# Gated linear attention and an MLP mixer on one core: transposes by crossbar DMA, inputs by casting DMA

## The chip, the cores and the metric

The kernel runs on one core of a Trainium2 chip. The metric is device time in microseconds (us), from one launch of the whole program. The core has TensorE (PE, matmuls, and its weight loads PEld), VectorE (DVE), ScalarE (ACT), GpSimd (POOL) and SyncE (SP). SP does nothing here but issue DMAs by the hardware queue; POOL issues DMAs by the software queue and also computes. All DMAs of the core run on the same 16 DMA engines.

## What is computed

For each of 4 batches and 8 heads, with S = 768 steps and head size D = 48, a gated recurrence runs over the steps, and its output, with the heads side by side (768 x 384), goes through an MLP mixer over tokens and then over channels:

```
f = 1 / (1 + exp(-f_logit))
for t in range(S):
    state = f[t][:, None] * state + outer(k[t], v[t])      # 48 x 48 per head
    y[t]  = q[t] @ state
x  = y with heads side by side                             # 768 x 384 per batch
u  = x + (relu(x.T @ w_tok1) @ w_tok2).T                   # w_tok1 768 x 256, w_tok2 256 x 768
out = u + relu(u @ w_ch1) @ w_ch2                          # w_ch1 384 x 1536, w_ch2 1536 x 384
```

All inputs and the output are float32 in memory.

## The kernel before

The recurrence is done in chunks of 128 steps, so NCH = 6 chunks per batch, steps on the partitions. Within a chunk the gates become a cumulative sum S of log(1 + exp(-f_logit)), and q and k are scaled by exp(-S) and exp(S); what remains is a masked product inside the chunk plus a term from the state carried in.

**Loads.** `load_batch_inputs(b, 1)` (L75) issues, for each chunk, four DMAs of 128 x 8 heads x 48 float32 (1024 rows of 192 bytes each) on SP: f_logit, q, k and v. v goes to one float32 staging tile `v_ld` and is cast to bf16 by POOL (L81). The four MLP weights are loaded whole by POOL (L62 to L65), which casts them to bf16 on the way. The order in the program is batch 0, weights, batch 1 (L298 to L300); batch b + 2 is loaded after batch b's attention (L328). `q_sb`, `k_sb`, `f_sb`, `v_sb` and the log gates `Lhi`, `Llo` (the high and low bf16 halves of the log gate) have two buffers each, by the batch's parity.

**Gates.** `prep_gates_slices` (L118) makes exp, ln and the high half on ACT (L124, L127, L130), and the low half on DVE (L133). Batch 0 does it chunk by chunk (L302 to L304). Batches 1 to 3 do it for all six chunks in one, a step after each of the chunks 1 to 4 of the batch ahead (L322).

**Attention.** `attn_front` (L137) makes the cumulative sum of a chunk in PSUM (`ps_S`, two matmuls) and the chunk's total (`ps_dg`). `attn_chunk` (L153) then takes exp of it both ways on ACT (`G`, `Gi`, L159, L160), scales q on DVE to `qh` (L164) and k on POOL to `kh` (L165). Both are 128 steps x 8 heads x 64 (48 used). PE transposes them in pairs of heads, 4 + 4 blocks of 128 x 128, into the PSUM tile `ps_tr` (L169, L170), and DVE copies the eight blocks to `qkT` in one instruction (L171). The scores `ps_AT` (L176) and their mask `AmT` (L185, L186) follow, then the output `ps_y` (L189, L195), the state's update (`ps_dg` L200, L209 to L215; it reads `kh` as it is, not transposed), and two copies of `ps_y` to `x_nat` (float32) and `x_bf` (L205, L206). `G`, `Gi`, `qh`, `kh`, `qkT` and `AmT` have two buffers by the chunk's parity; `ps_S` and `ps_y` have one.

**MLP.** `moe_slices(b)` (L223) gives six slices for batch b. They are called one each inside the chunks of batch b + 1 (L182), and those of batch 3 at the end: `s_tok` (token mixing, ends with `u_nat` L241 and its bf16 copy `u_bf` L242), `s_ut` (transposes `u_bf`, 18 blocks of 128 x 128, through `ps_moe` and three DVE copies to `uT`, L253 to L255), three times `s_ch` (channel expansion, L265, with the relu on ACT or DVE, L272, L270) and `s_out` (L283, L286, and the store on SP, L287). `ps_moe` has two buffers, and every MLP matmul group uses them.

**Order.** The program gives what depends on what. The tile framework's scheduler sets the order of each engine's instructions at compile time, from its own estimate of their lengths and from their place in the program; at run time each engine, and each of the queues of SP and POOL, works strictly in that order, and waits on semaphores.

Of the kernel before, what the change touches and what calls it, by code (L numbers as in the profile page):

```python
# [9 lines left out]
FP32 = mybir.dt.float32  # L10
BF16 = mybir.dt.bfloat16
_DBG = False
AF = mybir.ActivationFunctionType
ALU = mybir.AluOpType
# [3 lines left out]
def kernel(  # L18
# [12 lines left out]
    nc = tc.nc  # L31
    B, H, S, D = q.shape
    C = 128
    NCH = S // C
    HP = H // 2
# [7 lines left out]
    def st(shape, dtype, tag):  # L43
        return sb.tile(shape, dtype, tag=tag, name=tag)

    def pt(shape, dtype, tag):
        return ps.tile(shape, dtype, tag=tag, name=tag)

    tri_bf = st([128, 128], BF16, "tri_bf")
    ident = st([128, 128], BF16, "ident")  # L50
# [13 lines left out]
        nc.gpsimd.dma_start(out=w_ch1, in_=moe_w_ch1.rearrange("(kt p) n -> p kt n", p=128))  # L64
        nc.gpsimd.dma_start(out=w_ch2, in_=moe_w_ch2.rearrange("(kt p) n -> p kt n", p=128))  # L65

    q_sb = [st([128, H, NCH, D], FP32, f"q_sb{i}") for i in range(2)]
    k_sb = [st([128, H, NCH, D], FP32, f"k_sb{i}") for i in range(2)]
    v_ld = [st([128, H, NCH, D], FP32, "v_ld")] * 2
    v_sb = [st([128, H, NCH, D], BF16, f"v_sb{i}") for i in range(2)]  # L70
    f_sb = [st([128, H, NCH, D], FP32, f"f_sb{i}") for i in range(2)]
    Lhi = [st([128, NCH, H, 64], BF16, f"Lhi{i}") for i in range(2)]
    Llo = [st([128, NCH, H, 64], BF16, f"Llo{i}") for i in range(2)]

    def load_batch_inputs(b, step):  # L75
        i = b % 2
        for c in range(0, NCH, step):
            for dst, src in ((f_sb, f_logit), (q_sb, q), (k_sb, k), (v_ld, v)):
                nc.sync.dma_start(out=dst[i][:, :, c:c + step, :],
                                  in_=src[b].rearrange("h (c t) d -> t h c d", t=C)[:, :, c:c + step, :])  # L80
            nc.gpsimd.tensor_copy(v_sb[i][:, :, c:c + step, :], v_ld[i][:, :, c:c + step, :])  # L81

    G = [st([128, H, 64], BF16, f"G{i}") for i in range(2)]
    Gi = [st([128, H, 64], BF16, f"Gi{i}") for i in range(2)]
    qh = [st([128, H, 64], BF16, f"qh{i}") for i in range(2)]
    kh = [st([128, H, 64], BF16, f"kh{i}") for i in range(2)]
# [15 lines left out]
    nc.vector.memset(state_bd, 0.0)  # L102

    ps_S = pt([128, 512], FP32, "ps_S")
    ps_tr = pt([128, 8, 128], BF16, "ps_tr")
    ps_AT = [pt([128, 4, 128], FP32, f"ps_AT{p}") for p in range(2)]
    ps_y = pt([128, H, D], FP32, "ps_y")
    ps_dg = pt([128, HP, 2 * D + 1], FP32, "ps_dg")
# [9 lines left out]
    def prep_gates_slices(b, c0=0, c1=NCH):  # L118
        ib = b % 2
        fb = f_sb[ib][:, :, c0:c1, :]  # L120
        fbc = f_sb[ib].rearrange("t h c d -> t c h d")[:, c0:c1]

        def g_exp():
            nc.scalar.activation(fb, fb, AF.Exp, bias=0.0, scale=-1.0)  # L124

        def g_ln():
            nc.scalar.activation(fb, fb, AF.Ln, bias=1.0, scale=1.0)  # L127

        def g_hi():
            nc.scalar.activation(Lhi[ib][:, c0:c1, :, 0:D], fbc, AF.Copy, bias=0.0, scale=1.0)  # L130

        def g_lo():
            nc.vector.tensor_tensor(Llo[ib][:, c0:c1, :, 0:D], fbc,  # L133
                                    Lhi[ib][:, c0:c1, :, 0:D], ALU.subtract)
        return [g_exp, g_ln, g_hi, g_lo]
# [17 lines left out]
    def attn_chunk(b, c, mid=(), front_next=None):  # L153
        i = c % 2
        ib = b % 2
        last = c == NCH - 1

        sview = ps_S.rearrange("t (h dd) -> t h dd", dd=64)[:, :, 0:D]
        nc.scalar.activation(G[i][:, :, 0:D], sview, AF.Exp, bias=0.0, scale=-1.0)  # L159
        nc.scalar.activation(Gi[i][:, :, 0:D], sview, AF.Exp, bias=0.0, scale=1.0)  # L160
        if not last:
            nc.scalar.activation(glast, ps_dg[:, :, 2 * D], AF.Exp, bias=0.0, scale=-1.0)

        nc.vector.tensor_tensor(qh[i][:, :, 0:D], q_sb[ib][:, :, c, :], G[i][:, :, 0:D], ALU.mult)  # L164
        nc.gpsimd.tensor_tensor(kh[i][:, :, 0:D], k_sb[ib][:, :, c, :], Gi[i][:, :, 0:D], ALU.mult)  # L165

        qb, kb = blk(qh[i]), blk(kh[i])
        for hp in range(HP):
            nc.tensor.transpose(ps_tr[:, hp, :], qb[:, hp, :], ident)  # L169
            nc.tensor.transpose(ps_tr[:, 4 + hp, :], kb[:, hp, :], ident)  # L170
        nc.vector.tensor_copy(qkT[i], ps_tr)  # L171

        for h in range(H):
            hp, par = h // 2, h % 2
            rows = slice(par * 64, par * 64 + D)
            nc.tensor.matmul(ps_AT[par][:, hp, :], lhsT=qkT[i][rows, 4 + hp, :],  # L176
                             rhs=qkT[i][rows, hp, :], start=True, stop=True)

        if front_next is not None:
            front_next()  # L180
        for m in mid:
            m()  # L182

        tb4 = tri_bf.unsqueeze(1).broadcast_to((128, 4, 128))
        nc.vector.tensor_tensor(AmT[i][:, 0:4, :], ps_AT[0], tb4, ALU.mult)  # L185
        nc.vector.tensor_tensor(AmT[i][:, 4:8, :], ps_AT[1], tb4, ALU.mult)  # L186

        for h in range(H):
            nc.tensor.matmul(ps_y[:, h, :], lhsT=AmT[i][:, (h % 2) * 4 + h // 2, :],  # L189
                             rhs=v_sb[ib][:, h, c, :],  # L190
                             start=(h == 0), stop=(c == 0 and h == H - 1),
                             skip_group_check=True)
        if c > 0:
            for hp in range(HP):
                nc.tensor.matmul(ps_y[:, 2 * hp:2 * hp + 2, :], lhsT=qkT[i][:, hp, :],  # L195
                                 rhs=state_bd[:, hp, :],
                                 start=False, stop=(hp == HP - 1), skip_group_check=True)
        if not last:
            for hp in range(HP):
                nc.tensor.matmul(ps_dg[:, hp, 0:2 * D], lhsT=kb[:, hp, :],  # L200
                                 rhs=v_sb[ib][:, 2 * hp:2 * hp + 2, c, :],
                                 start=True, stop=True)

        yflat = ps_y.rearrange("t h e -> t (h e)")
        nc.scalar.activation(x_nat[ib][:, c, :], yflat, AF.Copy, bias=0.0, scale=1.0)  # L205
        nc.scalar.activation(x_bf[ib][:, c, :], yflat, AF.Copy, bias=0.0, scale=1.0)  # L206

        if not last:
            nc.vector.tensor_tensor(state[0:D], state[0:D], ps_dg[0:D, :, 0:D], ALU.add)  # L209
            nc.vector.tensor_tensor(state[64:64 + D], state[64:64 + D],  # L210
                                    ps_dg[64:64 + D, :, D:2 * D], ALU.add)
            nc.vector.tensor_tensor(state, state, glast.unsqueeze(2).broadcast_to((128, HP, D)),  # L212
                                    ALU.mult)
            nc.vector.tensor_copy(state_bd[0:D, :, 0:D], state[0:D])
            nc.vector.tensor_copy(state_bd[64:64 + D, :, D:2 * D], state[64:64 + D])  # L215
# [7 lines left out]
    def moe_slices(b):  # L223
        ib = b % 2
# [22 lines left out]
        sl.append(s_tok)  # L247

        def s_ut():
            for dmb in range(3):  # L250
                pm = ps_moe[dmb % 2].bitcast(BF16)
                for stt in range(NCH):
                    nc.tensor.transpose(pm[:, stt * 128:(stt + 1) * 128],  # L253
                                        u_bf[:, stt, dmb * 128:(dmb + 1) * 128], ident)
                nc.vector.tensor_copy(uT[:, dmb, :], pm[:, 0:S])  # L255
            if _DBG:
                nc.sync.dma_start(out=dbg_uT[b], in_=uT)
        sl.append(s_ut)
# [32 lines left out]
    if _DBG:  # L291
# [2 lines left out]
        dbg_h1 = nc.dram_tensor("dbg_h1", (B, 128, 2, DM), BF16, kind="Internal").ap()  # L294
        dbg_uT = nc.dram_tensor("dbg_uT", (B, 128, 3, S), BF16, kind="Internal").ap()
        dbg_zT = nc.dram_tensor("dbg_zT", (B, 128, 12, S), BF16, kind="Internal").ap()
    nc.scalar.preload_act_table_set("natural_log_exp_and_others")
    load_batch_inputs(0, 1)  # L298
    load_weights()
    load_batch_inputs(1, 1)  # L300
    prev_moe: list = []
    for c in range(NCH):  # L302
        for g in prep_gates_slices(0, c, c + 1):
            g()  # L304
    for b in range(B):
        ib = b % 2
        attn_batch_begin(b)
        next_gates = prep_gates_slices(b + 1) if b + 1 < B else []
        if b == 0:
            attn_front(b, 0)  # L310
        for c in range(NCH):
            if c + 1 < NCH:
                fn = (lambda cc: (lambda: attn_front(b, cc)))(c + 1)
            elif b + 1 < B:
                fn = lambda: attn_front(b + 1, 0)
            else:
                fn = None
            mid = []
            if c < len(prev_moe):
                mid.append(prev_moe[c])  # L320
            attn_chunk(b, c, mid=mid, front_next=fn)
            if 1 <= c <= len(next_gates):  # L322
                next_gates[c - 1]()
        if _DBG:
            nc.sync.dma_start(out=dbg_x[b].rearrange("(c t) n -> t c n", t=C),
                              in_=x_nat[b % 2])
        if b + 2 < B:
            load_batch_inputs(b + 2, 1)  # L328
        prev_moe = moe_slices(b)
    for s in prev_moe:  # L330
        s()
# [30 lines left out]
```

## Time and profile before

| | us |
|---|---|
| median of the runs (2) | 257.42 |
| lowest, highest | 256.96, 257.89 |
| the profiled execution's own time | 257.89 |
| its span, first to last instruction | 256.1 |
| busy: PE, PEld | 194.3, 113.9 |
| busy: DVE, ACT, POOL | 151.7, 115.1, 39.5 |
| mean granted TensorE clock | 0.947 |

The profile is of one execution. It has the busy time of each engine, the span in 40 equal slices of 6.4 us (a digit is the busy share in tenths), the DMA queues, the costliest groups of instructions, and, on demand, the timeline of an engine, the instructions of one source line, and tables of busy time between given moments. An engine's row with a "q" (SPq, POOLq) is its queue of DMA issues. In a timeline line the first number is the start in us from the span's start, the second the length, and in brackets at the end stands the idle time ahead of it and what ended it. Names such as `kh_96` and `kh_97` are two buffers of one tile; `in_f_logit_dram` is an input.

### The profile page before, as it was taken

The page shows a single profiled execution, that of the slowest core. Times are in us where ns is not written, and L with a number is a line of the kernel's source. Part 1 is how long each engine was busy: PE and PEld are TensorE (multiplying, and loading weights), DVE is VectorE, ACT ScalarE, POOL GpSimd, SP SyncE. Part 2 cuts the span into 40 slices and gives each one's busy share as a digit, 9 for nine tenths or more (in the row PEclk, how much of TensorE's full clock was granted, in tenths as well). Part 3 has the DMA queues.
Part 4 walks back from the last instruction along what each step waited for, and adds up shares of the span by engine and source line. Part 5 has one row for each costly group of instructions (what it writes and reads, how often), then busy time and mean ns, then how long its engine had stood idle before and what let it go on. Part 6 is the DMA issues. An engine that isn't in the chain of part 4 may idle for free. (4 is left out here: it accounts for less than half of the span.)

```text
span 256.1 us, 4360 instructions
## 1 busy us (share of the span) xinstructions
PE 194.3 (76%) x1678; PEld 113.9 (44%) x1688; DVE 151.7 (59%) x321; ACT 115.1 (45%) x240; POOL 39.5 (15%) x60
## 2 busy tenths in 40 slices
PE   0300168676795885899988989999799999789994
PEld 0100036452342444566654546665466566344462
DVE  4200059894631499976699998438998842542231
ACT  4502055424469554491485976017465601635300
POOL 1420062401010242301222231001210100000000
PEclk9999999976897798589999999999999999999999
DMA  7999999999999998019999000121000012000022
GB/s 141 165 208 189 193 186 178 189 178 176 179 195 189 168 166 140 0 32 198 227 167 181 5 0 3 61 92 35 0 4 0 3 61 96 29 0 0 3 92 92
DMA packets 106324, 27.02 MB, mean 105 GB/s; under 512 B 100288, under 2 KB 105920, under 8 KB 106304
## 3 DMA queue, kind: packets, MB, share of 16 engines
q1 hardware_dynamic: 103296, 23.60, 52.2%
q0 software_dynamic: 3008, 3.15, 7.2%
q8 instruction: 13, 0.21, 0.3%
q14 instruction: 7, 0.06, 0.1%
HBM read 25.17 MB, written 4.72 MB: 117 GB/s over the span
## 5 line engine op out<-in xcount | busy, mean ns | idle before, releaser
L265 PEld LDWEIGHTS <-w_ch_75 128*128 128x128 bf16 x288 | 27.9, 100 | 31.5 <-issue 17.9
L265 PE MATMUL ps_moe_135<-uT,w_ch_75 128*128 128x384 bf16 x144 | 33.6, 340 | 6.2 <-ACT zT L272 2.3
L283 PEld LDWEIGHTS <-zT 128*128 128x128 bf16 x288 | 27.7, 98 | 18.3 <-issue 0.3
L265 PE MATMUL ps_moe_136<-uT,w_ch_75 128*128 128x384 bf16 x144 | 34.3, 337 | 1.7 <-ACT zT L272 1.3
L283 PE MATMUL ps_moe_135<-w_ch_76,zT 128*128 128x384 bf16 x144 | 25.9, 326 | 0.1
L272 ACT ACTIVATE zT<-ps_moe_136 128x384 bf16<-128x384 f32 x32 | 15.8, 494 | 22.1 <-PE ps_moe_136 L265 21.8
L283 PE MATMUL ps_moe_136<-w_ch_76,zT 128*128 128x384 bf16 x144 | 25.7, 326 | 0.0
L133 DVE TENSOR_TENSOR Llo_88<-f_sb_84,Lhi_86 128x384 bf16<-128x384 f32 (+1 forms) x7 | 5.9, 841 | 25.4 <-ACT Lhi_86 L130 25.4
L272 ACT ACTIVATE zT<-ps_moe_135 128x384 bf16<-128x384 f32 x32 | 15.9, 496 | 10.9 <-PE ps_moe_135 L265 10.5
L205 ACT ACTIVATE x_nat_106<-ps_y 128x384 f32<-128x384 f32 x12 | 5.9, 491 | 24.9 <-PE ps_y L195 24.8
L270 DVE TENSOR_SCALAR zT<-ps_moe_136 128x384 bf16<-128x384 f32 x16 | 8.9, 554 | 12.9 <-PE ps_moe_136 L265 12.9
L286 DVE TENSOR_TENSOR out_sb_134<-u_nat,ps_moe_136 128x384 f32<-128x384 f32 x12 | 6.6, 553 | 15.6 <-PE ps_moe_136 L283 13.6
L141 PE MATMUL ps_S<-Lhi_86,tri_bf 128*128 128x512 bf16 x10 | 4.6, 461 | 14.4 <-ACT Lhi_86 L130 13.8
L205 ACT ACTIVATE x_nat_105<-ps_y 128x384 f32<-128x384 f32 x12 | 6.0, 498 | 20.6 <-PE ps_y L195 20.1
L124 ACT ACTIVATE f_sb_84<-f_sb_84 128x384 f32<-128x384 f32 (+1 forms) x7 | 5.2, 749 | 21.1 <-DMA f_sb_84<-in_f_logit_dram 21.1
L286 DVE TENSOR_TENSOR out_sb_133<-u_nat,ps_moe_135 128x384 f32<-128x384 f32 x12 | 6.6, 554 | 13.4 <-PE ps_moe_135 L283 13.4
L242 ACT ACTIVATE u_bf<-u_nat 128x384 bf16<-128x384 f32 x24 | 12.0, 522 | 4.3 <-DVE u_nat L241 3.8
L170 PE MATMUL ps_tr<-ident,kh_96 128*128 128x128 bf16 x48 | 8.1, 242 | 7.6 <-POOL kh_96 L165 7.6
L81 POOL CAST v_sb_82<-v_ld 128x384 bf16<-128x384 f32 x12 | 6.4, 536 | 29.6 <-DMA v_ld<-in_v_dram 29.6
L165 POOL TENSOR_TENSOR kh_97<-k_sb_80,Gi_93 128x384 bf16<-128x384 f32 x6 | 5.5, 909 | 35.5 <-ACT Gi_93 L160 28.8
L148 PE MATMUL ps_dg<-ones_bf,Lhi_86 128*128 128x1 bf16 x40 | 3.6, 166 | 9.3 <-ACT Lhi_86 L130 8.1
L270 DVE TENSOR_SCALAR zT<-ps_moe_135 128x384 bf16<-128x384 f32 x16 | 8.9, 554 | 2.6 <-PE ps_moe_135 L265 2.4
(122 smaller groups left out, 431.5 us busy)
## 6 DMA issues: line engine op xcount, KB each, us to landing
v_ld<-in_v_dram SPq DMA_DIRECT2D x24, 192.0 KB, 4.5
f_sb_84<-in_f_logit_dram SPq DMA_DIRECT2D x12, 192.0 KB, 4.6
q_sb_77<-in_q_dram SPq DMA_DIRECT2D x12, 192.0 KB, 4.8
k_sb_79<-in_k_dram SPq DMA_DIRECT2D x12, 192.0 KB, 4.7
f_sb_85<-in_f_logit_dram SPq DMA_DIRECT2D x12, 192.0 KB, 4.7
q_sb_78<-in_q_dram SPq DMA_DIRECT2D x12, 192.0 KB, 4.7
k_sb_80<-in_k_dram SPq DMA_DIRECT2D x12, 192.0 KB, 4.4
out_dram<-out_sb_133 SPq DMA_DIRECT2D x12, 192.0 KB, 1.9
```

What stands on the lines that cost most here:

```text
L81: nc.gpsimd.tensor_copy(v_sb[i][:, :, c:c + step, :], v_ld[i][:, :, c:c + step, :])
L124: nc.scalar.activation(fb, fb, AF.Exp, bias=0.0, scale=-1.0)
L133: nc.vector.tensor_tensor(Llo[ib][:, c0:c1, :, 0:D], fbc, Lhi[ib][:, c0:c1, :, 0:D], ALU.subtract)
L165: nc.gpsimd.tensor_tensor(kh[i][:, :, 0:D], k_sb[ib][:, :, c, :], Gi[i][:, :, 0:D], ALU.mult)
L170: nc.tensor.transpose(ps_tr[:, 4 + hp, :], kb[:, hp, :], ident)
L205: nc.scalar.activation(x_nat[ib][:, c, :], yflat, AF.Copy, bias=0.0, scale=1.0)
L242: nc.scalar.activation(u_bf[:, stt, :], u_nat[:, stt, :], AF.Copy, bias=0.0, scale=1.0)
L265: nc.tensor.matmul(pm[:, 0:384], lhsT=w_ch1[:, kt, cc * 128:(cc + 1) * 128], rhs=uT[:, kt, th * 384:(th + 1) * 384], start=(kt == 0), stop ...
L270: nc.vector.tensor_scalar(dst, pm[:, 0:384], 0.0, None, ALU.max)
L272: nc.scalar.activation(dst, pm[:, 0:384], AF.Relu, bias=0.0, scale=1.0)
L283: nc.tensor.matmul(pm[:, 0:DM], lhsT=zT[:, kt, tt * 128:(tt + 1) * 128], rhs=w_ch2[:, kt, :], start=(kt == 0), stop=(kt == 11))
L286: nc.vector.tensor_tensor(o, u_nat[:, tt, :], pm[:, 0:DM], ALU.add)
```

## The change

Four things change together.

1. The transposes of `qh` and `kh` are two crossbar DMAs per chunk on SP, each 128 x 512 bf16 from SBUF to SBUF, straight into `qkT`; those of `u_bf` are six crossbar DMAs per batch, each 128 x 384, straight into `uT`. The PE transposes, `ps_tr` and the DVE copies go.
2. q, k and v are loaded by POOL's queue, cast to bf16 on the way; only f_logit stays on SP. Batch 0 is still loaded by chunks; batches 1 to 3 are one DMA per tensor. The POOL casts of v go. The weights are loaded after batches 0 and 1.
3. The scaling of k (L165) moves from POOL to DVE.
4. Batch 0's gates are made for chunk 0 and then for chunks 1 to 5 in one, and the line that loads one activation table set ahead of all else is taken out.

```diff
-    q_sb = [st([128, H, NCH, D], FP32, f"q_sb{i}") for i in range(2)]
-    k_sb = [st([128, H, NCH, D], FP32, f"k_sb{i}") for i in range(2)]
-    v_ld = [st([128, H, NCH, D], FP32, "v_ld")] * 2
+    q_sb = [st([128, H, NCH, D], BF16, f"q_sb{i}") for i in range(2)]
+    k_sb = [st([128, H, NCH, D], BF16, f"k_sb{i}") for i in range(2)]
...
-    def load_batch_inputs(b, step):
+    def load_batch_inputs(b, c0=0, c1=NCH):
         i = b % 2
-        for c in range(0, NCH, step):
-            for dst, src in ((f_sb, f_logit), (q_sb, q), (k_sb, k), (v_ld, v)):
-                nc.sync.dma_start(out=dst[i][:, :, c:c + step, :],
-                                  in_=src[b].rearrange("h (c t) d -> t h c d", t=C)[:, :, c:c + step, :])
-            nc.gpsimd.tensor_copy(v_sb[i][:, :, c:c + step, :], v_ld[i][:, :, c:c + step, :])
+        if (c0, c1) == (0, NCH):
+            nc.gpsimd.dma_start(out=q_sb[i], in_=q[b].rearrange("h (c t) d -> t h c d", t=C))
+            nc.gpsimd.dma_start(out=k_sb[i], in_=k[b].rearrange("h (c t) d -> t h c d", t=C))
+            nc.gpsimd.dma_start(out=v_sb[i], in_=v[b].rearrange("h (c t) d -> t h c d", t=C))
+            nc.sync.dma_start(out=f_sb[i], in_=f_logit[b].rearrange("h (c t) d -> t h c d", t=C))
+            return
+        for c in range(c0, c1):
+            nc.sync.dma_start(out=f_sb[i][:, :, c, :],
+                              in_=f_logit[b].rearrange("h (c t) d -> t h c d", t=C)[:, :, c, :])
+            nc.gpsimd.dma_start(out=q_sb[i][:, :, c, :],
+                                in_=q[b].rearrange("h (c t) d -> t h c d", t=C)[:, :, c, :])
...
-        nc.gpsimd.tensor_tensor(kh[i][:, :, 0:D], k_sb[ib][:, :, c, :], Gi[i][:, :, 0:D], ALU.mult)
+        nc.vector.tensor_tensor(kh[i][:, :, 0:D], k_sb[ib][:, :, c, :], Gi[i][:, :, 0:D], ALU.mult)
...
-        for hp in range(HP):
-            nc.tensor.transpose(ps_tr[:, hp, :], qb[:, hp, :], ident)
-            nc.tensor.transpose(ps_tr[:, 4 + hp, :], kb[:, hp, :], ident)
-        nc.vector.tensor_copy(qkT[i], ps_tr)
+        nc.sync.dma_start_transpose(out=qkT[i][:, 0:4, :],
+                                    in_=qh[i].rearrange("t h dd -> t (h dd)"))
+        nc.sync.dma_start_transpose(out=qkT[i][:, 4:8, :],
+                                    in_=kh[i].rearrange("t h dd -> t (h dd)"))
...
-            for dmb in range(3):
-                pm = ps_moe[dmb % 2].bitcast(BF16)
-                for stt in range(NCH):
-                    nc.tensor.transpose(pm[:, stt * 128:(stt + 1) * 128],
-                                        u_bf[:, stt, dmb * 128:(dmb + 1) * 128], ident)
-                nc.vector.tensor_copy(uT[:, dmb, :], pm[:, 0:S])
+            for stt in range(NCH):
+                nc.sync.dma_start_transpose(out=uT[:, :, stt * 128:(stt + 1) * 128],
+                                            in_=u_bf[:, stt, :])
...
-    nc.scalar.preload_act_table_set("natural_log_exp_and_others")
-    load_batch_inputs(0, 1)
+    load_batch_inputs(0, 0, 2)
+    load_batch_inputs(0, 2, NCH)
+    load_batch_inputs(1)
     load_weights()
-    load_batch_inputs(1, 1)
     prev_moe: list = []
-    for c in range(NCH):
-        for g in prep_gates_slices(0, c, c + 1):
-            g()
+    for g in prep_gates_slices(0, 0, 1) + prep_gates_slices(0, 1, NCH):
+        g()
...
-            load_batch_inputs(b + 2, 1)
+            load_batch_inputs(b + 2)
```

More of the change, by code (lines that the diff above doesn't have):

```diff
@@ L73 @@
     Llo = [st([128, NCH, H, 64], BF16, f"Llo{i}") for i in range(2)]
-    def load_batch_inputs(b, step):
+    def load_batch_inputs(b, c0=0, c1=NCH):
         i = b % 2
-        for c in range(0, NCH, step):
-            for dst, src in ((f_sb, f_logit), (q_sb, q), (k_sb, k), (v_ld, v)):
-                nc.sync.dma_start(out=dst[i][:, :, c:c + step, :],
-                                  in_=src[b].rearrange("h (c t) d -> t h c d", t=C)[:, :, c:c + step, :])
-            nc.gpsimd.tensor_copy(v_sb[i][:, :, c:c + step, :], v_ld[i][:, :, c:c + step, :])
+        if (c0, c1) == (0, NCH):
[9 more added lines that the diff above has]
+                                in_=q[b].rearrange("h (c t) d -> t h c d", t=C)[:, :, c, :])
+            nc.gpsimd.dma_start(out=k_sb[i][:, :, c, :],
+                                in_=k[b].rearrange("h (c t) d -> t h c d", t=C)[:, :, c, :])
+            nc.gpsimd.dma_start(out=v_sb[i][:, :, c, :],
+                                in_=v[b].rearrange("h (c t) d -> t h c d", t=C)[:, :, c, :])
     G = [st([128, H, 64], BF16, f"G{i}") for i in range(2)]
@@ L104 @@
     ps_S = pt([128, 512], FP32, "ps_S")
-    ps_tr = pt([128, 8, 128], BF16, "ps_tr")
     ps_AT = [pt([128, 4, 128], FP32, f"ps_AT{p}") for p in range(2)]
```

## The prediction

> **What bounds the kernel now.** I read the slices of the page first, then the timelines of SP, ACT, DVE and PE for the places where they change, then a table of busy time by stages.
>
> ```profile
> span 256.1 us, 4360 instructions
> ...
> PE   0300168676795885899988989999799999789994
> ...
> PEclk9999999976897798589999999999999999999999
> DMA  7999999999999998019999000121000012000022
> ```
>
> DMA is full for 16 slices of 6.4 us, about 97 us; from slice 16 on PE is. The stages (columns: stretch, its length, then busy us and count for PE, PEld, DVE, ACT, POOL, the clock, DMA share, GB/s), cut where a batch's attention or MLP ends:
>
> ```profile
> 0.00:33.00 33.00, 4.13 (x23) 1.33 (x23) 5.29 (x20) 8.17 (x16) 6.32 (x16) 1.00 1.07 179
> 33.00:60.00 27.00, 19.09 (x222) 13.17 (x224) 22.76 (x53) 12.82 (x32) 8.49 (x12) 0.92 1.15 182
> 60.00:124.40 64.40, 53.04 (x429) 30.00 (x431) 40.14 (x77) 34.58 (x62) 11.87 (x18) 0.82 0.90 147
> 124.40:172.20 47.80, 43.67 (x421) 26.49 (x422) 37.27 (x76) 26.56 (x57) 8.25 (x10) 1.00 0.45 85
> 172.20:216.80 44.60, 41.98 (x407) 25.91 (x409) 33.80 (x74) 20.48 (x51) 4.55 (x5) 1.00 0.08 28
> 216.80:256.10 39.30, 32.40 (x185) 16.98 (x183) 12.42 (x23) 12.49 (x26) 0.00 (x0) 1.00 0.10 35
> ```
>
> Rows 1 and 2 (batch 0's attention, over at 60) wait for loads. Row 3 (MLP of batch 0, attention of batch 1) has 11.4 us without PE work. Rows 4 and 5 are PE-bound (91 and 94%). Row 6 is the last MLP alone. Why rows 1 and 3 wait:
>
> ```profile
> 0.74 1.28 ACT L297 ACT_TABLE_LOAD   x1 [0.74 <-PEq L346]
> 10.55 9.55 SPq L79 DMA_DIRECT2D k_sb_79<-in_k_dram  x1
> 32.61 0.91 POOL L165 TENSOR_TENSOR kh_96<-k_sb_79,Gi_92 128x384 bf16<-128x384 f32 x1
> 35.35 0.69 DVE L171 COPY qkT_98<-ps_tr 128x1024 bf16<-128x1024 bf16 x1
> 75.02 2.12 ACT L124 ACTIVATE f_sb_85<-f_sb_85 128x2304 f32<-128x2304 f32 x1
> 88.57 0.23 PE L170 MATMUL ps_tr<-ident,kh_96 128*128 128x128 bf16 x1 [0.54 <-POOL kh_96 L165]
> 88.63 0.22 PE L169 MATMUL ps_tr<-ident,qh_94 128*128 128x128 bf16 x1
> 224.96 0.56 DVE L255 COPY uT<-ps_moe_135 128x768 bf16<-128x768 bf16 x1
> ```
>
> The weights (issued by POOL from 7.4) push the loads back: one SP issue lasts 9.55 us. The first `kh` comes at 32.61, the first `qkT` at 35.35. Batch 1's gates start only at 75.02, since its f_logit was last loaded at 67, so its transposes come at 88. A PE transpose costs 57 ns (88.57 to 88.63), not its 219.
>
> **What the Trainium skill says.** "VectorE: DVE Perf Modes", The three transpose paths: a full 128x128 bf16 transpose takes 390 ns on TensorE and 1309 ns by the DMA crossbar. The trace has 57 ns in a row of PE transposes, so the PE side is cheaper than that; no run here shows the crossbar. "DMA: Bandwidth & Descriptors", Latency and other measured facts: a DMA transpose moves 261 GB/s in one kernel. Its section Issuing engines are not separate DMA queues: all queues share the 16 engines, and interleave. The trace agrees: the weights slowed SP's loads. "ScalarE: Activation LUTs", What ACT_TABLE_LOAD costs: 1283 ns and about 1380 of drain at each switch of set. The trace has 1.28 us, once.
>
> **PE and DVE relief.** Removed are 24 x 8 + 4 x 18 = 264 PE transposes x 57 ns = 15 us, of which each PE-bound batch has 66, 3.8 us. At row 3's clock of 0.82 it is 4.6. DVE loses 24 x 0.69 + 12 x 0.56 = 23.3 us of copies and gains 24 scalings of k: 0.28 to 0.56 us each (the 0.556 of q's scaling, halved if the bf16 inputs run at double rate), at most 13.3. POOL loses 24 x 0.91 + 24 x 0.51 and gains some 30 issues of about 1 us. DVE (59% busy) and POOL (15%) bound nothing, so both stand at nothing; if a chunk were bound by DVE the extra 0.56 us would count 24 times, 13 us.
>
> **The transposing DMA.** Two prices for 128x512: 1.3 us, plus 96 KB more at 261 GB/s, is 1.7 us; four times 1.3 is 5.2. I take 1.7, as most of so small a DMA should be fixed cost, and keep 5.2. For 128x384: 1.55 (or 3.9). To land I add 1.5 (a store of 192 KB, all told, lands in 1.9). From `kh` to `qkT` that makes 2 x 1.7 + 1.5 = 4.9 us, against 35.35 + 0.69 - 33.52 = 2.5 before.
>
> **Start.** A 1024-row load takes 1.1 us (SP's 52 issues from 40.9 to 97.9). SP now has six chunks of f_logit and one whole batch, 12 such loads, ahead of the first transpose; POOL has 18 for batch 0 beside them. Sharing the engines, SP's 12 are through at 12 x 1.1 x 2 = 26.4, so the first `qkT` lands at 27 + 4.9 = 32, 4 us sooner than the 36.0 of before. Then a chunk takes about 5 us (the pair of 3.4, half longer by POOL's loads beside it) against 4.05 ((55.61 - 35.35)/5). The sixth `qkT` is at 57, the batch over at 62, against 60. The casting loads I price as the plain ones, 1.1 us per 1024 rows; twice that is kept as the other end, since the rows written shrink to 96 bytes.
>
> **Weights last.** They start behind batch 1's q, k, v: 18 + 18 loads x 1.1 + 13 of f is 54 us. Their packets (7.2% of 256.1, 18.4 us) end at 73. `w_tok1` is needed at 62 and is there at about 58; `w_ch1` at 67 is hidden behind `s_tok` and `s_ut`. If the loads cost double, this cover is gone.
>
> **Gates of batch 1.** f_logit lands by 27 instead of 69, so attention 1 runs beside MLP 0 at once, and up to the 11.4 us of row 3's idle is gained.
>
> **The last transposes.** `u_bf` pieces appear from 220.7 to 223.5. Six x 1.55 in a row plus 1.5 gives 231.5, where `uT` was whole at 225.5: +6. Inside batches 1 to 3 two of q's and k's own transposes may stand between on SP (3.4), so +7, of which one chunk's PE work covers some 2.5: +4.5. Stores and the next f_logit (6.6 us whole, for two batches) are on SP's queue too: whatever is behind a waiting transpose waits.
>
> **Table loads.** Nothing now asks for one set with both exp and ln. If each ln needs its own, five gate groups give 10 more switches, 1.28 to 2.66 us each; if not, none. I take the 10. Four lie ahead of the first transpose, hidden by its wait until 27. Each of batches 1 to 3's gates costs 2.6 to 5.3 on ACT, which also empties `ps_moe`; PE then stalls for some 3.5, as DVE takes only a third of the relus.
>
> **Waits of `qkT`.** 2.4 us more for each of 18 chunks; MLP matmuls fill most. I put 2 per batch.
>
> **Sum.** Rows 1 and 2: 62. Row 3: 64.4 - 11.4 - 4.6 + 4.5 + 3.5 + 2 = 58.4. Row 4: 47.8 - 3.8 + 10 = 54. Row 5: 44.6 - 3.8 + 10 = 50.8. Row 6: 39.3 + 6 = 45.3. Together 270.5, against 256.1. The profiled run is 1.8 over its span (257.89), and within 0.5 of the median 257.42, so 272.
>
> **Rivals.**
> Relief wins: SP runs ahead, static order fills all gaps, and ACT keeps one set. Then 60 + 48.4 + 44 + 40.8 + 42 = 235, so 237. For it speaks that PE is 91 to 94% busy in rows 4 and 5 and that row 3's hole is due to late gates; against it, a strictly ordered SP queue. The point that decides is whether the 10 us per batch that I add for u, tables and `qkT` stay under about 3.
> SP's stream becomes the bound: at 5.2 and 3.9 us, 27 + 48 x 5.2 + 24 x 3.9 + the 30.5 from `uT` to the end is 401. Per batch SP needs 12 x 1.7 + 6 x 1.55 + 6.6 + 2 (stores) = 38 us at my price, already near PE's 41; it decides from about 2.1 us per transpose on.
> Slow casting loads: at 2.2 us per 1024 rows, batches 0 and 1 take 36 x 2.2 + 13 = 92, the first weight comes at 95 instead of 58. MLP 0 then begins 33 us later with attention 1 done, which gives back about 15: 290.
> The change doesn't do what it says (a transpose element by element): 65,536 elements each would cost milliseconds; the diff names the crossbar form, so I leave it out.
>
> **From cases to numbers.** Mine (258 to 292) 0.53; relief wins (232 to 252) 0.18; slow casting loads (280 to 310) 0.16; SP's stream (310 to 410) 0.13. The range 237 to 315 leaves about 0.08 below and 0.12 above. My own case alone is 258 to 292. About 2% is what a measurement can tell from no change, 252.3 to 262.6. Faster by more: 0.18. Within: a tenth, the lower edge of mine, 0.10. Slower: 0.72.
>
> **What would show it.** First `qkT` read near 32. Transpose DMAs of 1.7 us on SP and landing within 3.5; `uT` whole 8 us after the last `u_nat`. Eleven table loads, in pairs about each ln. Batch 1's gates ahead of 60. PE with holes at `s_ch`'s start in each batch. The prediction is wrong if SP's transposes issue in well under 1 us and PE stays over 90% after 60 (faster), or if SP's queue is full all through (far slower).

## The result: 287.3 us, slower by 11.6%

| | before | after |
|---|---|---|
| median, us | 257.42 | 287.27 (287.23 to 287.31, 2 runs) |
| ratio to before, 95% interval | | 1.116 (1.107 to 1.125) |
| span of the profiled execution | 256.1 | 285.2 |
| busy: PE, DVE, ACT, POOL | 194.3, 151.7, 115.1, 39.5 | 182.9, 134.7, 126.6, 40.1 |
| mean granted TensorE clock | 0.947 | 0.910 |

The direction was forecast, and 287 lies inside the range; the size was not: +30 us instead of +14.5. Where the runs of a kernel fall into two groups (f6 below), its faster run is compared. The slices of the profile after, beside those shown of before:

```profile
span 285.2 us, 3835 instructions
...
PE   0104414006465558499993989988289989379994
...
PEclk9999999999655869899997899999979999958999
DMA  9999999999999969990389222233531122210022
```

PE is short of work for the first 17 slices of 7.1 us, and the eighth and ninth are a hole. DMA is full in 16 of these 17. The stages, cut where the ones of before were (end of batch 0's attention, then of each MLP; columns as before):

```profile
0.00:90.70 90.70, 27.15 (x244) 14.83 (x248) 34.39 (x79) 51.44 (x64) 31.28 (x35) 0.91 1.78 157
90.70:143.90 53.20, 42.43 (x330) 23.65 (x332) 33.69 (x74) 22.41 (x53) 6.63 (x3) 0.87 1.23 101
143.90:192.90 49.00, 41.03 (x350) 24.05 (x352) 28.28 (x68) 20.75 (x51) 2.21 (x1) 0.93 0.64 79
192.90:240.60 47.70, 39.35 (x333) 23.04 (x332) 27.31 (x67) 20.26 (x50) 0.00 (x0) 0.96 0.30 66
240.60:285.20 44.60, 32.97 (x163) 16.56 (x162) 11.08 (x21) 11.70 (x25) 0.00 (x0) 0.89 0.15 45
```

| stage | before | forecast | after |
|---|---|---|---|
| batch 0's attention | 60.0 | 62 | 90.7 |
| MLP 0, attention 1 | 64.4 | 58.4 | 53.2 |
| MLP 1, attention 2 | 47.8 | 54 | 49.0 |
| MLP 2, attention 3 | 44.6 | 50.8 | 47.7 |
| MLP 3 | 39.3 | 45.3 | 44.6 |

The first stage is 28.7 us longer than forecast, the other four together 14.0 shorter: 270.5 + 28.7 - 14.0 = 285.2. So the question is batch 0's attention: the miss there is twice the net one of 14.7, and the shorter stages behind it hide half. From the timelines of SP and PE:

```profile
9.51 10.00 SPq L176 DMA_TRANSPOSE qkT_97<-qh_93  x1
19.62 1.27 SPq L178 DMA_TRANSPOSE qkT_97<-kh_95  x1
22.92 0.70 SPq L80 DMA_DIRECT2D f_sb_83<-in_f_logit_dram  x1
28.73 4.27 SPq L176 DMA_TRANSPOSE qkT_98<-qh_94  x1
35.81 1.25 SPq L178 DMA_TRANSPOSE qkT_97<-kh_95  x1
37.53 0.70 SPq L80 DMA_DIRECT2D f_sb_84<-in_f_logit_dram  x1
44.09 4.37 SPq L176 DMA_TRANSPOSE qkT_98<-qh_94  x1
66.05 0.50 PE L240 MATMUL ps_moe_133<-x_bf_106,w_tok_73 128*128 128x384 bf16 x1 [19.85 <-DMA w_tok_73<-in_moe_w_tok_dram]
88.88 0.60 PE L184 MATMUL ps_AT_122<-qkT_97 48*128 48x128 bf16 x4 [3.60 <-DMA qkT_97<-kh_95]
```

The first transpose holds SP for 10 us behind the f_logit loads. Between the first transposes SP also issues f_logit of batches 2 and 3, two whole batches, and the first transpose behind each holds SP for 4.3 and 4.4 us; the others shown issue in 1.3. At 46.2 PE stops: its fixed order has the first matmul of token mixing there, in the middle of batch 0's attention, and `w_tok1` lands at 66.05. After that PE waits for `qkT` again. How long the crossbar DMAs take from issue to landing (last number, median us), first between 28 and 60 us, then between 150 and 230 us:

```profile
qkT_98<-qh_94 SPq DMA_TRANSPOSE x2, 10.2
qkT_98<-kh_96 SPq DMA_TRANSPOSE x2, 7.3
qkT_97<-qh_93 SPq DMA_TRANSPOSE x2, 6.8
qkT_97<-kh_95 SPq DMA_TRANSPOSE x2, 6.9
```

```profile
qkT_98<-qh_94 SPq DMA_TRANSPOSE x5, 2.4
qkT_98<-kh_96 SPq DMA_TRANSPOSE x5, 2.4
qkT_97<-qh_93 SPq DMA_TRANSPOSE x4, 2.5
qkT_97<-kh_95 SPq DMA_TRANSPOSE x4, 2.5
```

The same DMA takes 2.4 us with the engines nearly free and 7 to 10 beside loads (in the slowest of these medians SP's hold of over 4 us is part of it). Two theories stood: the late `w_tok1` (A), and the crossbar DMAs themselves (B).

### The profile page after: what moved, and what is told of

The parts are those of the page before. It is cut to its first block, busy times and chain, and to the rows that moved or that the text cites. A ratio compares the mean times of both kernels' runs of the same rounds, so it can differ in the third digit from the quotient of the medians.

```text
span 285.2 us, 3835 instructions
## 1 busy us (share of the span) xinstructions
PE 182.9 (64%) x1412; PEld 102.1 (36%) x1424; DVE 134.7 (47%) x305; ACT 126.6 (44%) x238; POOL 40.1 (14%) x39
## 3 DMA queue, kind: packets, MB, share of 16 engines
q1 hardware_dynamic: 50448, 18.10, 35.3%
## 4 chain that ended last, share of the span: by engine, by line
PE 44%; DMA 23%; ACT 9%; DVE 8%; another core or an unknown queue 7%; SPq 5%; issue 2%; DVEq 0%; ACTq 0%
DMA qkT_97<-kh_95 9%; PE ps_moe_133 L270 9%; PE ps_moe_134 L270 8%; PE ps_moe_134 L288 7%; PE ps_moe_133 L288 6%; SPq L176 4%; DMA qkT_98<-kh_96 3%; DMA uT<-u_bf 3%; PE ps_AT_122 L184 3%; DMA qkT_97<-qh_93 2%; DMA qkT_98<-qh_94 2%; PE ps_y L197 2%; PE ps_S L149 2%; DVE Llo_88 L141 2%
## 5 line engine op out<-in xcount | busy, mean ns | idle before, releaser
L270 PEld LDWEIGHTS <-w_ch_75 128*128 128x128 bf16 x288 | 28.4, 104 | 41.7 <-issue 29.1
L270 PE MATMUL ps_moe_133<-uT,w_ch_75 128*128 128x384 bf16 x144 | 36.3, 365 | 9.1 <-DMA uT<-u_bf 6.8
L270 PE MATMUL ps_moe_134<-uT,w_ch_75 128*128 128x384 bf16 x144 | 34.9, 354 | 5.6 <-DMA uT<-u_bf 5.3
L288 PE MATMUL ps_moe_133<-w_ch_76,zT 128*128 128x384 bf16 x144 | 25.5, 326 | 1.3 <-DVE out_sb_131 L291 1.1
L277 ACT ACTIVATE zT<-ps_moe_133 128x384 bf16<-128x384 f32 x32 | 15.8, 494 | 23.1 <-PE ps_moe_133 L270 22.9
L277 ACT ACTIVATE zT<-ps_moe_134 128x384 bf16<-128x384 f32 x32 | 15.7, 492 | 21.9 <-PE ps_moe_134 L270 21.3
L288 PE MATMUL ps_moe_134<-w_ch_76,zT 128*128 128x384 bf16 x144 | 25.4, 326 | 0.0
L217 DVE TENSOR_TENSOR state<-state,ps_dg 48x192 f32<-48x192 f32 x20 | 6.8, 340 | 30.4 <-PE ps_dg L208 24.0
L275 DVE TENSOR_SCALAR zT<-ps_moe_133 128x384 bf16<-128x384 f32 x16 | 8.9, 557 | 21.5 <-PE ps_moe_133 L270 21.3
L240 PE MATMUL ps_moe_133<-x_bf_106,w_tok_73 128*128 128x384 bf16 x12 | 4.0, 417 | 20.8 <-DMA w_tok_73<-in_moe_w_tok_dram 19.9
L184 PE MATMUL ps_AT_122<-qkT_97 48*128 48x128 bf16 x48 | 6.3, 261 | 16.2 <-DMA qkT_97<-kh_95 12.4
L167 ACT ACTIVATE G_89<-ps_S 128x384 bf16<-128x384 f32 x12 | 5.9, 488 | 23.4 <-remote 19.5
L193 DVE TENSOR_TENSOR AmT_99<-ps_AT_122,tri_bf 128x512 bf16<-128x512 f32 x12 | 8.3, 690 | 14.0 <-PE ps_AT_122 L184 10.2
L240 PEld LDWEIGHTS <-w_tok_73 128*128 128x128 bf16 x48 | 4.7, 106 | 25.0 <-DMA w_tok_73<-in_moe_w_tok_dram 20.1
L141 DVE TENSOR_TENSOR Llo_87<-f_sb_83,Lhi_85 128x384 bf16<-128x384 f32 (+2 forms) x3 | 5.3, 1758 | 14.7 <-ACT Lhi_85 L138 14.7
```

The lines of the kernel that those rows point to most:

```text
L141: nc.vector.tensor_tensor(Llo[ib][:, c0:c1, :, 0:D], fbc, Lhi[ib][:, c0:c1, :, 0:D], ALU.subtract)
L240: nc.tensor.matmul(pm[:, 0:DM], lhsT=w_tok1[:, kt, rt * 128:(rt + 1) * 128], rhs=x_bf[ib][:, kt, :], start=(kt == 0), stop=(kt == NCH - 1))
L270: nc.tensor.matmul(pm[:, 0:384], lhsT=w_ch1[:, kt, cc * 128:(cc + 1) * 128], rhs=uT[:, kt, th * 384:(th + 1) * 384], start=(kt == 0), stop ...
L275: nc.vector.tensor_scalar(dst, pm[:, 0:384], 0.0, None, ALU.max)
L277: nc.scalar.activation(dst, pm[:, 0:384], AF.Relu, bias=0.0, scale=1.0)
L288: nc.tensor.matmul(pm[:, 0:DM], lhsT=zT[:, kt, tt * 128:(tt + 1) * 128], rhs=w_ch2[:, kt, :], start=(kt == 0), stop=(kt == 11))
```

## The experiments

Each kernel is the changed one with the edit named, unless it says otherwise. "Twin" is the same kernel with all transposes on TensorE. To place a gain, the start of the first relu of token mixing (`h1T`) is given: it stands just behind batch 0's attention (before: 60.7; after: 92.1).

### First set: the weights, the transposes, the old loads

e1, the weights ahead of batch 1's inputs:

```diff
-    load_batch_inputs(1)
     load_weights()
+    load_batch_inputs(1)
```

> The changed kernel with one edit: the four weights are issued ahead of batch 1's q, k, v. Theory A (late weights: TensorE's fixed order has token-mixing matmuls inside batch 0's attention, and the one at 46 us stands still until w_tok1 lands at 66): the 19.85 us hole goes, batch 0's attention ends near 70 instead of 90.7, and the time falls by 12 to 20 us to 267 to 275, less if batch 1's q, k, v, now behind the weights, are late in turn. Theory B (the crossbar DMAs, which land in 6 to 7 us beside loads, and the table loads set batch 0's pace): another wait takes the place of the hole, and the time stays above 282.

e2, only `w_tok1` moved there:

> The changed kernel with one edit: only w_tok1 is issued ahead of batch 1's q, k, v; the other three weights stay last. Theory A: the matmul at 46 us waits for w_tok1 alone, so this does as well as moving all four, or better since batch 1's inputs are delayed by only some 2.5 us: 265 to 275. If instead it is the whole bulk of bytes ahead of the MLP that matters, the hole moves to w_tok2 or w_ch1 and less than half is gained: 278 to 285.

e4, the twin of the change (lines 169 to 171 and 250 to 255 of the kernel before put back in place of the crossbar DMAs):

> The changed kernel with all transposes put back on TensorE with their PSUM copies; loads, order, table loads and the scaling of k as changed. Theory A: the wait for w_tok1 stays, at least 10 us of it, and only the 5.5 us at the end, some 1 to 3 us per batch and the 6 us landings in batch 0 are won: 268 to 278. Theory B (the crossbar transposes are the loss): back to 252 to 262.

e5, the kernel before with the crossbar DMAs in place of its transposes, nothing else changed:

> The kernel before with one edit: all transposes by crossbar DMA on SP; loads, weights early, POOL's scaling of k and the one table load as before. Theory A says nothing of late weights here (they land by 32 us), and its other half, a strictly ordered SP queue, says that the first transposes stand behind the 48 loads of batches 0 and 1 on SP, which are issued by 67 us: batch 0's attention starts at 67 instead of 33, and the time is 285 to 305. If the queue's order does not matter and only the transposes' own cost does: 262 to 272.

Measured: e1 290.9 us, ratio to before 1.133 (1.127 to 1.140); e2 291.7, 1.134 (1.130 to 1.138); e4 251.2, 0.976 (0.969 to 0.982); e5 299.9, 1.169 (1.163 to 1.176).

Theory A as I had put it fell: e1 and e2 were not faster. But they had not taken the wait away (14.3 us of it stayed in e2). From e1's table of waits (total, times, longest, in us):

```profile
PE ps_moe L240 <- DMA w_tok<-in_moe_w_tok_dram: 22.1, 1, 22.1
```

Issued at 26.9 in e1 instead of 54.8, the `w_tok` loads took 23.8 us (median of the two) to land instead of some 12. e4 gave back 36 us and beat the kernel before, although it too has the wait, shorter:

```profile
58.11 0.82 PE L241 MATMUL ps_moe<-x_bf,w_tok 128*128 128x384 bf16 x2 [12.29 <-DMA w_tok<-in_moe_w_tok_dram]
```

So the rest of the change (the loads and their order, k's scaling on DVE, the gates) is a gain by itself, and the crossbar transposes are worth more than the whole loss. e5 did as the strictly ordered SP queue says: its first crossbar DMA stands behind all 48 loads.

```profile
64.38 0.96 SPq L79 DMA_DIRECT2D v_ld<-in_v_dram  x1
65.44 1.74 SPq L167 DMA_TRANSPOSE qkT<-qh  x1
```

Its first `h1T` is at 98.6 instead of 60.7. In this kernel, crossbar transposes on SP need the loads moved to another queue, as the change does with q, k and v; f_logit it leaves ahead of them.

### Second set: which transposes, which traffic, which table loads

e3, the line that loads one activation table set put back:

> The changed kernel with one edit: the activation table set with both exp and ln is loaded ahead of all else again, so one table load instead of 11. The trace of the change has 10 loads more of 1.28 us each. My prediction put 3.5 us for each of three batches on the path, 10 in all: then 275 to 279. If they are covered (ACT is 44% busy, and six of the ten fall in the first 46 us, where loads are awaited): 284 to 288.

f2, only u's transposes back on TensorE:

> The changed kernel with the transposes of u alone put back on TensorE; those of q and k stay crossbar DMAs. Theory C (the crossbar DMAs of q and k, 24 pairs, which land in 6 to 8 us beside casting loads and in 2.4 alone, are what TensorE waits for; those of u cost the 5.5 us of the last MLP and about 3 in each of three others): 270 to 277. Theory D (u's six DMAs in a row on SP, 7.7 us ahead of each channel expansion, are the bulk of the 36 us that putting all transposes back won): 255 to 265.

f3, and its twin f4, leave out later loads:

```diff
-    q_sb = [st([128, H, NCH, D], BF16, f"q_sb{i}") for i in range(2)]
+    q_sb = [st([128, H, NCH, D], BF16, "q_sb")] * 2
...
-            nc.gpsimd.dma_start(out=q_sb[i], in_=q[b].rearrange("h (c t) d -> t h c d", t=C))
```

and the same for k and v.

> The changed kernel without the loads of q, k and v for batches 1 to 3: these batches compute on batch 0's q, k and v. f_logit, weights and all else are as in the change. To be read against the same with TensorE transposes. Theory C (the crossbar DMAs are slow because they share the 16 engines with casting loads): without these loads they land in 2.5 us, and crossbar costs only 8 to 16 us over TensorE transposes, about 250 to 258 here. Theory E (a crossbar transpose costs the same with or without loads: its 2 x 1.2 us of issue, its 2.4 us of flight, and SP's fixed order): 24 us or more, 265 or more here.

> The kernel with changed loads and TensorE transposes (251 us), without the loads of q, k and v for batches 1 to 3, which compute on batch 0's. With batch 1's loads gone the weights land by about 40 us, the 12.3 us wait for w_tok1 goes, and 238 to 244 is left. If the wait for w_tok1 was covered by other work, 246 to 251.

Measured: e3 286.0, 1.114 (1.110 to 1.118); f2 272.7, 1.061 (1.057 to 1.064); f3 272.2, 1.061 (1.055 to 1.067); f4 244.0, 0.948 (0.946 to 0.950).

e3: the ten extra table loads are covered, as the second half of its expectation said; its 1.3 us are within the noise. f2, where its theory C had it, splits the 36 us by place. Its first `h1T` is at 91.8, as in the change, and what follows takes 179.4 us, against 193.1 in the change and 177.2 in e4. So after batch 0 u's transposes cost 13.7 us and those of q and k 2.2; within batch 0 those of q and k cost 20.

f3 came out as theory E had said, not C: without later q, k and v the crossbar still costs 28 us. But E also said that traffic makes no difference, and f3 does not show that, as other traffic took the place of what was left out. Its `h1T` starts at 87.6, its twin's at 66.3, so 21 of the 28 lie in batch 0 again. There the weights were in flight instead, and the wait for `w_tok1` stayed although batch 1's loads were gone (f4 kept 8.5 us of it, so its time fits the first forecast but not for the reason given). The two `w_tok` loads, issued within 0.3 us of the same moment in both, took twice as long beside crossbar DMAs; first f3's, then f4's line of the DMA issues:

```profile
w_tok<-in_moe_w_tok_dram POOLq DMA_DIRECT2D x2, 384.0 KB, 25.0
```

```profile
w_tok<-in_moe_w_tok_dram POOLq DMA_DIRECT2D x2, 384.0 KB, 12.5
```

And between 36 and 44 us, with all four weights in flight in both and no f_logit moving, the software queue, which carries the weights, moved 0.85 MB in f3 (first line) and 1.69 in f4 (second):

```profile
q0 software_dynamic: 1099, 0.85, 103.8%
```

```profile
q0 software_dynamic: 1036, 1.69, 115.6%
```

Beside them f3's hardware queue moved 0.26 MB of crossbar DMAs; with these, all engines came to 138 GB/s against 213 in f4. From 44 to 52 us, when a last crossbar DMA trickled in f3, the weights moved 1.23 MB in both.

So here the slowing is mutual. That made theory F: traffic draws a crossbar DMA out, and a crossbar DMA slows that traffic.

### Third set: hardly any traffic

f5 and its twin f6 also leave out the weights' loads, filling the four tiles instead:

```diff
-        nc.gpsimd.dma_start(out=w_tok1, in_=moe_w_tok1.rearrange("(kt p) n -> p kt n", p=128))
+        nc.gpsimd.memset(w_tok1, 0.01)
```

> Crossbar transposes with as little other DMA traffic as the program allows: q, k and v are loaded for batch 0 only and reused, and the four weights are not loaded but filled with a constant by POOL. To be read against the same with TensorE transposes. Theory F (a crossbar DMA is drawn out by traffic beside it, from 2.4 us to as much as 18, and slows that traffic too; 22 of the 28 us that crossbar cost without later loads came before the end of batch 0's attention, while the weights were in flight): the difference of the pair falls to 6 to 13 us, about 248 to 256 here. Theory E (issue, flight and fixed order cost the same without traffic): the difference stays at 20 us or more, 260 or more here.

> The pair's other half: the same loads left out and weights filled with a constant, all transposes on TensorE. The 8.5 us wait for w_tok1 of the kernel that still loads weights goes: 234 to 242. POOL's fills could be a wait of their own; then 242 to 246.

e8 and e10 are twins with the table line put back, e8 also with the weights ahead of batch 1:

> A version to beat both kernels: the changed loads and order, with TensorE transposes, the weights ahead of batch 1's q, k, v, and one activation table set. Against the 251 us with the weights last and 11 table loads: the 12.3 us wait for w_tok1 shrinks to what was left without batch 1's loads (8.5), and table loads come off the gates: 243 to 249. If batch 1's inputs are then late, 249 to 254.

> As the 251 us version (changed loads and order, TensorE transposes, weights last) with one activation table set. With TensorE transposes ACT is nearer the path of batches 1 to 3 than it was with crossbar ones, where one set gained about 1 us: 246 to 250. If table loads are covered here too: 250 to 252.

Measured: f5 256.6, 1.000 (0.995 to 1.006); f6 239.1 in one run and 244.9 to 245.2 in three, so without a ratio; e8 249.5, 0.971 (0.967 to 0.975); e10 246.3, 0.957 (0.954 to 0.961).

What is left beside the crossbar DMAs in f5 is batch 0's q, k and v, all of f_logit and the stores. Its `h1T` starts at 71.6, 16 us sooner than f3's, and between 28 and 60 us its crossbar DMAs landed in less than in the change (6.8 to 10.2):

```profile
qkT<-qh SPq DMA_TRANSPOSE x4, 5.0
qkT<-kh SPq DMA_TRANSPOSE x4, 3.0
```

f5 is 17.5 us above the faster run of f6, between the forecasts of F (6 to 13) and E (20 or more). So of the 36 us between the change and its twin, 8 went with the later q, k and v and 10.6 more with the weights; 17.5, about half, stayed with hardly any traffic. (The split is rough: it rests on one run of f6, and POOL's fills hold up both kernels, as shown below.) Part of what stayed is f_logit's: in f5, too, the transposes behind its whole loads held SP for 4.3 and 4.7 us, the second when nothing but f_logit and crossbar DMAs moved. No run takes f_logit off SP's queue, so its share is open.

f6's profiled run is one of the slower ones and a poor measure by places: its PE waits 13.8 us for `qh`, and ahead of `qh` a copy on DVE that takes 0.25 us elsewhere lasts until just after POOL's last fill.

```profile
24.89 12.16 DVE L220 CAST state_bd<-state 48x192 bf16<-48x192 f32 x1
32.95 4.00 POOL L65 MEMSET w_ch<- 128x4608 bf16 x1
```

In f5 the same copy lasts 8.45 us and ends with the fills as well, at 37.2.

### Fourth set: is the wait for w_tok1 a loss by itself?

g1 puts all weights ahead of all inputs, g2 is its twin, g3 the twin with one table set; g4 is e10 with `w_tok1` alone ahead of all inputs. h1 is the change with that last edit alone, h2 its twin:

```diff
+    nc.gpsimd.dma_start(out=w_tok1, in_=moe_w_tok1.rearrange("(kt p) n -> p kt n", p=128))
     load_batch_inputs(0, 0, 2)
```

with that load taken out of `load_weights`.

> The changed kernel with one edit: the four weights are issued ahead of all inputs. The wait for w_tok1 must go. Theory A (the wait by itself cost 12 to 20 us): 267 to 276, batch 0's attention ending near 75. Theory F (the crossbar DMAs drawn out by whatever traffic is beside them set batch 0's pace; the wait hid part of that): batch 0's inputs, now 18 us later behind the weights, are loaded beside the crossbar DMAs until about 75, its attention ends at 85 or later, and the time is 280 to 290.

> The same with all transposes on TensorE, the pair of the one above. If traffic beside crossbar DMAs is the cause, the pair differs by 20 to 30 us (casting loads of all batches are still beside them, the weights are not), that is 255 to 265 here as batch 0 starts later than in the 251 us version; if the wait for w_tok1 was the cause, by 10 to 16.

> As the one above, with one activation table set. One set gained 5 us with the weights last: 249 to 261, 4 to 6 below its twin.

> The 246 us version (TensorE transposes, changed loads, one table set) with w_tok1 alone issued ahead of all inputs, the other weights last. The 15.8 us wait for w_tok1 goes, batch 0 starts some 3 us later: 234 to 242. If the wait only covered others (w_tok2 and w_ch1 are still late, and batch 1 is not ready sooner): 243 to 249.

> The changed kernel with one edit: w_tok1 alone is issued ahead of all inputs. If the wait for w_tok1 is a loss by itself: batch 0's attention ends near 75 and the time is 268 to 276. If the crossbar DMAs, drawn out beside the loads, set the pace and the wait only hid them: attention ends at 85 or later, 280 to 288.

> Its twin with all transposes on TensorE and 11 table loads: the twin with one table load took 239, the table gained 2 to 5 elsewhere, so 241 to 245. The pair then differs by 27 to 33 if the wait is a loss by itself, by 36 to 46 if not.

Measured: g1 287.6, 1.121 (1.115 to 1.127); g2 254.4, 0.987 (0.983 to 0.992); g3 252.3, 0.980 (0.978 to 0.983); g4 239.1, 0.930 (0.926 to 0.934); h1 283.5, 1.103 (1.097 to 1.109); h2 239.3, 0.930 (0.928 to 0.932).

As expected on theory F, g1 and h1 have no wait on PE for `w_tok1` and gain little or nothing. g1 gains nothing, but it starts batch 0 late; h1 has not that excuse and gains 3.8 us, where its twin gains 12 (251.2 to 239.3, more than the 241 to 245 forecast). In h1's waits, over the whole program, the place of the weight is taken by the crossbar (the change has 26.5 of this wait):

```profile
PEld L183 <- DMA qkT<-kh: 40.2, 12, 10.7
```

The pair h1, h2 differs by 44 us, more than the change and its twin; g1 and g2 differ by 33, above the 20 to 30 forecast. So with crossbar transposes the wait for `w_tok1` mostly covered waits for `qkT`; with TensorE transposes it was a loss of its own. The differences of the pairs in the profiled executions (crossbar less TensorE, us), cut at each MLP's first `h1T`:

| beside the crossbar DMAs | to MLP 0 | MLP 0 | MLP 1 | MLP 2 | MLP 3 | sum |
|---|---|---|---|---|---|---|
| all loads, weights late (change, e4) | 20.3 | 2.1 | 4.3 | 4.6 | 5.0 | 36.3 |
| all loads, w_tok1 first (h1, h2) | 25.0 | 8.9 | 2.3 | 5.3 | 4.1 | 45.5 |
| all loads, weights first (g1, g2) | 15.2 | 7.4 | 5.1 | 5.4 | 3.7 | 36.7 |
| weights, no later q, k, v (f3, f4) | 21.3 | -1.5 | -0.3 | 4.9 | 4.5 | 28.8 |
| neither (f5, f6) | 3.5 | -0.3 | 1.5 | 5.4 | 4.3 | 14.4 |

The last two columns hardly change (3.7 to 5.4): a price that does not depend on the traffic left out. By f2 it is mostly u's six DMAs in a row, 3.3 of the 4.6 in MLP 2 and all of MLP 3. The columns ahead of them vary with the traffic. The row of f5 and f6 is distorted by POOL's fills, and f6's profiled run is 6 us above its fastest, so the sum there is nearer 17.5 and the 3.5 is not a measure of batch 0.

The best version of all is h2 or g4, 7% faster than the kernel before: the changed loads, TensorE transposes and `w_tok1` first. The table line makes no difference there (239.3 and 239.1); between g2 and g3 it made 2.1, where 4 to 6 were forecast.

## Why the prediction was right or wrong

**The step that failed** is Start: "Then a chunk takes about 5 us (the pair of 3.4, half longer by POOL's loads beside it) ... the batch over at 62". The first pair landed at 25.6, sooner than the 32 said. But then a chunk took (90.2 - 28.5)/5 = 12.3 us from output to output, not 5. The wait for `w_tok1` is in this; h1, without it, still took (85.7 - 30.6)/5 = 11.0, and its twin on TensorE 6.4. Beside loads a crossbar DMA was not half longer but 3 to 4 times (7 to 10 us against 2.4), and it slowed the loads it shared the engines with; that the loads would pay too was not in the sum at all. I took the skill's sentence, in Issuing engines are not separate DMA queues of "DMA: Bandwidth & Descriptors", that all queues interleave on the 16 engines, as a fair share; the runs show a worse bargain (weights at half the rate beside crossbar DMAs, f3 against f4). That 287 lies in the range, and near the 290 of the rival with slow casting loads, is luck: the range was made wide for other causes.

**Weights last.** The loads of the weights were to start at 54 (the sum as written gives 52.6), and did at 54.8. `w_tok1` was to be there at 58; it took 11.2 us to land, at 66. That f_logit of batches 2 and 3 goes out at 22.9 and 37.5, I missed; what it did to the landing no run shows. "Needed at 62" was wrong as well: PE's order needs it at 46. In this kernel that miss is worth only 3.8 us (h1), in its twin 12.

**Price of a transpose.** 1.7 us of issue was taken, 1.2 measured, for 128 x 512 and 128 x 384 alike; 1.5 more to land, 1.2 measured (2.4 in all). The upper end of 5.2 and with it the rival of SP's stream is out. The skill's 1309 ns for one 128 x 128 block ("VectorE: DVE Perf Modes", The three transpose paths) is near the 1.2 us of issue that four blocks in one DMA cost here, with 2.4 to landing.

**Table loads.** Eleven, in pairs about each ln, 1.28 us each, as forecast. The 10.5 us of stall were not there: one set gained 1.3 us here (e3, within the noise), 5 in the twin with late weights, 2 with the weights first, nothing with `w_tok1` first. What they cost depends on what else is awaited at the time.

**The last transposes.** +6 for the last MLP was said, +5.3 measured; +4.5 in each other batch. By f2 u's transposes cost 13.7 us after batch 0, against 19.5 in the sum.

**Waits of `qkT`.** 2 per batch was said for batches 1 to 3; 2.2 measured for all three together (f2 against e4, one profiled execution each), so it was put too high.

**Gates of batch 1 and relief.** Right in direction: Lhi of batch 1 was made at 31.5, and MLP 0 with attention 1 fell from 64.4 to 53.2 (58.4 forecast), though some of attention 1 now lies in the longer stage ahead. DVE's busy time fell by 17.0 us, PE's by 11.4, unseen in the time.

**Casting loads.** The rival of double price is not what happened: the weights started at 54.8, where it had 95. The price itself is not settled. In e4 the 6144 rows of a batch landed in 9.0 us for v, but in 18.4 for k and 20.4 for q (medians of three), beside different other loads.

What stays open is why the two kinds of DMA hinder each other so; a crossbar DMA has many small packets (below), but no run varied them. The granted clock, 0.910 against 0.979 in e4, is lower in the change, but can be little of the 36 us: h1's two runs at the lowest clock (0.872 and 0.876) took 282.9 and 281.5 us, those at 0.926 and 0.946 took 285.5 and 284.2.

## What to carry to other kernels

A crossbar transpose can look hidden when priced alone; ask what else is on the DMA engines while its reader waits. Here it was drawn out by that traffic and slowed it, and whatever was strictly ordered behind the reader stopped too; roughly half of its cost followed the traffic, the other half stayed without it. When a wait is found, take it away without adding another before calling it the cause: of four ways of bringing the late weight forward two left the wait (e1, e2), one moved a delay elsewhere (g1), and the fourth (h1) showed that it mostly hid another wait. And when a change has several parts, time them apart: here the crossbar transposes were a loss of 14%, the rest a gain of 2%.

## What the runs showed of the hardware that was not expected

- A crossbar DMA from SBUF to SBUF held SP for 1.19 to 1.24 us and landed 2.3 to 2.5 us after its issue for 128 KB and for 96 KB alike, on engines nearly free. Beside loads its landing took up to 14.8 us in the change, with the 10.0 that it held SP, and 17.9 in f3, where the issue was 1.3.
- The hardware queue's packets are 50448 in the change and 14352 in e4, 36096 more for 72 crossbar DMAs. f2, which has only the 48 large ones, has 40464. So a DMA of 128 KB makes 544 packets and one of 96 KB 416, some 240 bytes each on average.
- Beside crossbar DMAs the same two weight loads took 25.0 us to land instead of 12.5 (f3, f4), and in the same 8 us the engines moved 138 GB/s instead of 213.
- While POOL filled four tiles (26.4 to 37.0 us in f6), a copy of 48 x 192 on DVE took 12.16 us instead of 0.25, and ended 0.1 us after the last fill.
